# The sixth product of the last two output quads on the second seven-product level

## The chip, the cores and the metric

The kernel runs on one core of a Trainium2 chip. The metric is device time in microseconds (us) of one execution; less is better. The core has a matrix engine (TensorE, PE in the profile, with its weight loads as PEld), a vector engine (VectorE, DVE), a scalar engine (ScalarE, ACT), GpSimd (POOL) and a queue engine (SyncE, SP) that issues most DMAs. Matrix products are accumulated in PSUM, eight banks of 512 float32 columns per partition; everything else lives in SBUF.

## The reference

A linear-attention block and then a token-mixing MLP, each behind a layer norm and with a residual; S = 2048 tokens, D = 1024 channels, F = 3584 hidden units:

```
h  = x + A(layernorm(x), wqkv, wo)                 # attention
u  = gelu(einsum("bsd,sf->bdf", LN(LN(h)), w1) + b1)   # first mixer
y  = einsum("bdf,fs->bds", u, w2) + b2             # second mixer
h2 = h + y.transpose(0, 2, 1)
```

The change is in the second mixer: a product of w2 transposed (2048 x 3584) with the gelu output g (3584 x 1024).

## The kernel before

**Tiling.** The 2048 output rows are 16 tiles of 128; two tiles form a pair p, handled by a `Mixer2` object (`st` in the code); two pairs form a `Quad`. There are four quads, u = 0 to 3. The 3584 hidden units are 14 steps k of two tiles of 128 (even and odd), the 1024 channels two halves of 512 columns.

**First level.** Each pair is a 2 x 2 block product (two row tiles, even and odd hidden tiles, two column halves), done with seven products instead of eight (`Product7`). Product m takes a left operand `lhs[m]` (128 x 128 per k, 14 of them) and a right operand (128 x 512 per k). Operands 1, 2 and 4 are blocks of w2, operands 5, 6, 7 and 3 are sums that VectorE makes (`asum(m)`, 1792 elements per partition): 5 = a21 + a22, 6 = operand 5 - a11, 7 = a11 - a21, 3 = a12 - operand 6. The right operand of product 6 is `gT2`, that of 7 and 4 are `gs` tiles in two halves, parked in DRAM and reloaded, or (second half of 4) made anew by `remake_t4`. In the accumulators: A = P1, then B = P1 + P6, C = B + P7, and so on; A becomes `t1`, a copy of it psB, a copy of that psC (`copy_c`).

**Second level.** Some products are done for both pairs of a quad at once, again as a 2 x 2 block product with seven inner products (`Inner`, and `Inner2`, whose results are added directly where they belong): the two pairs give the two block rows, the parity of k the inner dimension, two halves of 256 columns (HW) the block columns. An inner product is a block of seven matmuls of 256 columns. Its left operands are sums of 896 elements (`Inner.sums`, tiles `is`), its right operands sums of 1792 elements made once and kept (`inner_moving`, tiles `gi`). In quads 1 to 3 the products 1, 5, 2 and 3 are on the second level (stages in1, in5, in2, in3), while 6, 7 and 4 are plain: 14 matmuls of 512 columns for each pair.

**The order around the change.** `Quad.run2` writes out one quad by hand. `Quad.interleave` runs the seven inner products in the order i1, i6, i2, i5, i7, i3, i4 and puts matmuls of a plain product ("fills") between them at four cuts: the second half of the previous quad's product 4 in in1, product 6 in in5, product 7 in in2, the first half of product 4 in in3. At named points between them ("b" after i1, "c" after i6, "2", "7", "third", "end") it emits sums and loads, and flushes `late`, a list of evacuations. The fills cover the way from an inner product through PSUM: i1 is copied by ScalarE to the bank in which i6 accumulates, i6 to the bank for i7 (L273, L279); VectorE or ScalarE reads i2, i5, i7, i3 and i4 (the sinks).

TensorE and VectorE keep the program's order (`Held`, `pin`); ScalarE's order in this part is set by the scheduler. Each engine runs its own queue in order and waits on semaphores. SBUF pools with `reuse_waits="tile"` make a new tile wait only for the tiles whose place it takes. `load("in1")`, after in1, reloads the second half of product 7's `gs` and the odd w2 tiles of the next quad on the SP queue. Outputs go through `out`: an evacuation into one of four small tiles, then an accumulating DMA on POOL's queue.

Of the kernel before, what the change touches and what calls it, by code (L numbers as in the profile page):

```python
# [30 lines left out]
def kernel(  # L31
# [32 lines left out]
    const = ctx.enter_context(tc.tile_pool(name="const", bufs=1))  # L64
    actx_psum = ExitStack()
# [22 lines left out]
    ident = const.tile([P, P], BF16)  # L88
# [26 lines left out]
    b1_rows = const.tile([NF, P], BF16)  # L115
    b2_rows = const.tile([NS, P], BF16)
# [96 lines left out]

    def inner_moving(M, nk, pool, name):
        v = M.rearrange("p (k two) (h f) -> p k two h f", two=2, h=2)
        b11, b12, b21, b22 = v[:, :, 0, 0, :], v[:, :, 0, 1, :], v[:, :, 1, 0, :], v[:, :, 1, 1, :]
        t2, t3, t4 = (pool.tile([P, nk // 2, HW], FP16, name=f"{name}{t}")[:] for t in (2, 3, 4))
# [20 lines left out]
    class Inner:  # L238
# [220 lines left out]
    class Mixer2(Product7):  # L459
# [52 lines left out]
    class Quad:  # L512
# [29 lines left out]
        def interleave(self, n, steps, at={}, flush=(("7", None), ("end", None)), first=0):  # L542
            t = len(steps)
            cuts = [0, (5 * t + 8) // 16 + first, (9 * t + 8) // 16 + first, (12 * t + 8) // 16 + first, t]
# [12 lines left out]
            for f in (  # L557
                n.i1, "b", 0, n.i6, "c", n.i2, "2", 1, n.i5, n.i7, "7", 2, n.i3, "third", 3, n.i4, "end",
            ):
# [38 lines left out]
        def run2(self, rest, nxt, load, sums, cut, first):  # L598
            sts = self.sts

            def starting():
                self.in1.sums(slice(2, 4))
                self.asums(5)
                self.in5 = self.inner(5)
                self.in5.sums(slice(0, 2))
                sts[0].asum(6)
# [3 lines left out]

            def evac(s, dh, t):
                return lambda: sts[s].evac(0, dh, t[:, s, :])

            def every(*fs):
                return lambda: [f() for f in fs]

            def shared(st):
# [18 lines left out]

            def third():
# [1264 lines left out]
```

## Time and profile before

Three runs took 552.0, 552.32 and 553.42 us, median 552.32. The profiled execution took 552.11 us; its span, first to last instruction, is 550.3 us, at a granted TensorE clock of 1.00.

| stretch of the span (us) | what runs | PE busy | DVE busy | ACT busy |
|---|---|---|---|---|
| 0 to 385 | attention, first mixer | 382.80 | 322.63 | 249.47 |
| 385 to 422.19 | quad 0 (plain but product 5) | 37.19 | 33.60 | 6.96 |
| 422.19 to 464.74 | quad 1 | 42.55 | 37.19 | 10.48 |
| 464.74 to 504.26 | quad 2 | 39.52 | 28.26 | 11.53 |
| 504.26 to 547.01 | quad 3 and the last fills | 42.75 | 30.99 | 11.79 |
| 547.01 to 550.3 | last outputs | 0.00 | 0.58 | 0.00 |

The page gives busy times, a chain of the work that ended last, and groups of instructions; the timeline lists instructions in order of time, runs of equal ones merged. Matmul lengths in it are modelled and overlap, so the time a block takes is read from the start of the next one. A VectorE instruction overlaps the next one as well: its price in a full queue is the distance between starts.

### The profile page before, as it was taken

Reading aid. Unit: us, or ns where it says so; the run is one execution under the profiler, and the core shown is the slowest. Engines: PE = TensorE matmul, PEld = TensorE weight load, DVE = VectorE, ACT = ScalarE, POOL = GpSimd, SP = SyncE. Lnnn points to the kernel's source line nnn. Section 1 sums busy time; section 2 is a strip of 40 time slices with the busy share of each in tenths; the row PEclk is TensorE's granted clock in tenths of the full one; section 3 lists DMA queues with packets and bytes.
Section 4 is the critical chain, followed back from the end, with each engine's and each line's share of the span. In section 5 each row is a group of like instructions: output and inputs, shape, how many; then the busy total and the mean of one; then the engine's idle time right before and its main releaser. Section 6 shows DMA issues by size and latency. Waiting matters only on the chain.

```text
span 550.3 us, 9989 instructions
## 1 busy us (share of the span) xinstructions
PE 544.8 (99%) x3888; PEld 322.4 (59%) x3888; DVE 453.2 (82%) x881; ACT 290.2 (53%) x619; POOL 26.3 (5%) x36
## 2 busy tenths in 40 slices
PE   8999999999999999999999999999999999999997
PEld 3444446646634444456666766766455667667665
DVE  7798897865895999879988889888889979749747
ACT  5748677767788777635556465564220413413311
POOL 1000000000000000000000000000002103103111
PEclk9999999999999999999999999999999999999999
DMA  8933432205646981104041340422697749849334
GB/s 290 323 78 76 79 78 40 40 1 154 230 114 180 295 312 76 58 0 155 1 154 59 95 153 2 152 60 77 163 297 199 208 144 235 207 143 218 93 108 74
DMA packets 83151, 74.58 MB, mean 136 GB/s; under 512 B 15890, under 2 KB 74528, under 8 KB 83104
## 3 DMA queue, kind: packets, MB, share of 16 engines
q1 hardware_dynamic: 78720, 69.87, 43.0%
q0 software_dynamic: 4096, 3.68, 4.9%
q8 instruction: 30, 0.49, 0.4%
q10 hardware_dynamic: 288, 0.39, 0.2%
q14 instruction: 17, 0.14, 0.1%
HBM read 59.12 MB, written 11.67 MB: 129 GB/s over the span
## 4 chain that ended last, share of the span: by engine, by line
PE 96%; DVE 1%; DMA 1%; ACT 1%; issue 0%; ACTq 0%; DVEq 0%
PE psI L233 27%; PE psC L233 17%; PE acc_t L233 13%; PE psB L233 11%; PE psC L980 4%; PE psB L980 4%; PE psA L980 4%; PE psA L233 3%; PE acc_t L896 3%; PE psE L980 2%; PE acc_t L1315 2%; PE psA L1114 1%; PE psB L1114 1%; PE psC L1114 1%; PE kvps L926 1%; DMA x_sb<-in_A_x_dram 1%
## 5 line engine op out<-in xcount | busy, mean ns | idle before, releaser
L233 PEld LDWEIGHTS <-is 128*128 128x128 f16 x764 | 74.6, 98 | 32.1 <-DVE hi L233 0.4
L233 PEld LDWEIGHTS <-sa 128*128 128x128 f16 x683 | 66.8, 98 | 34.2
L233 PEld LDWEIGHTS <-wq 128*128 128x128 bf16 (+1 forms) x596 | 58.3, 98 | 38.8 <-issue 1.0
L233 PE MATMUL acc_t<-wo_sb,pqT 128*128 128x512 f16 x256 | 55.6, 379 | 0.0
L490 POOL DMA_DIRECT2D out_dram<-wq x28 | 24.4, 951 | 512.2 <-DMA wq<-in_B_w_dram 391.0
L233 PEld LDWEIGHTS <-pqT 128*128 128x128 bf16 x256 | 25.0, 98 | 30.5 <-issue 0.6
L233 PE MATMUL psC<-gs,wq 128*128 128x512 f16 x168 | 40.8, 379 | 0.0
L233 DVE TENSOR_TENSOR t<-psI,t 128x256 f32<-128x256 f32 (+1 forms) x45 | 20.8, 475 | 22.2 <-PE psI L233 20.9
L980 PEld LDWEIGHTS <-xs 128*128 128x128 f16 x208 | 20.0, 98 | 22.7
L233 PE MATMUL psC<-hT,sa 128*128 128x512 f16 x112 | 31.2, 379 | 0.0
L233 PE MATMUL psI<-hi,is 128*128 128x256 f16 x200 | 30.0, 273 | 0.0
L233 PE MATMUL psB<-hT,sa 128*128 128x512 f16 x112 | 29.7, 379 | 0.0
L233 PE MATMUL psC<-hT,wq 128*128 128x512 f16 x112 | 28.4, 379 | 0.0
L233 DVE BATCH_NORM_STATS2 hst<-acc_t 128x6 f32<-128x512 f32 x32 | 21.1, 690 | 6.9 <-ACT h_bf L233 6.9
L980 PE MATMUL psA<-wkv,xnT 128*128 128x512 bf16 x104 | 26.7, 379 | 0.0
L233 PE MATMUL psB<-gT,sa 128*128 128x512 f16 x112 | 26.5, 379 | 0.0
L980 PEld LDWEIGHTS <-xnT 128*128 128x128 bf16 x156 | 15.2, 98 | 18.1 <-issue 0.2
L233 DVE TENSOR_TENSOR e<-psI,es 128x256 f32<-128x256 f32 x22 | 9.3, 424 | 19.5 <-PE psI L233 19.5
L233 ACT CAST h_bf<-acc_t 128x512 bf16<-128x512 f32 x32 | 18.4, 583 | 12.4 <-PE acc_t L233 12.4
L233 ACT COPY psI<-psI 128x256 f32<-128x256 f32 x50 | 18.0, 360 | 11.6 <-PE psI L233 9.7
L193 DVE TENSOR_SCALAR e_sb<-e_sb 128x512 bf16<-128x512 bf16 x64 | 18.2, 284 | 7.2 <-ACT e_sb L188 7.0
L233 PE MATMUL psI<-gi,is 128*128 128x256 f16 x182 | 24.1, 273 | 0.0
(234 smaller groups left out, 1107.0 us busy)
## 6 DMA issues: line engine op xcount, KB each, us to landing
wq<-in_B_w_dram SPq DMA_DIRECT2D x14, 1024.0 KB, 7.5
wq<-in_B_w_dram SPq DMA_DIRECT2D x20, 448.0 KB, 5.8
gs<-parked SPq DMA_DIRECT2D x9, 896.0 KB, 4.7
shared_sb<-rd_dram SPq DMA_DIRECT2D x32, 128.0 KB, 3.8
out_dram<-h_bf SPq DMA_DIRECT2D x16, 256.0 KB, 3.6
x_sb<-in_A_x_dram SPq DMA_DIRECT2D x14, 256.0 KB, 4.0
w2o<-in_B_w_dram SPq DMA_DIRECT2D x4, 896.0 KB, 9.6
out_dram<-wq POOLq DMA_DIRECT2D x28, 128.0 KB, 4.7
```

Source lines behind the costliest of these rows:

```text
L193: pin(nc.vector.tensor_scalar(e_sb[:], e_sb[:], 1.0, PHI_EPS, ALU.min, ALU.add))
L233: return (lambda *a, **kw: pin(op(*a, **kw))) if self.always or getattr(Held, self.key) else op
L490: nc.gpsimd.dma_start(to, ot[:, a:b], accum_op=ALU.add)
L896: mm = nc.tensor.matmul(pp[:, 0:CW], lhsT=xnT[:, kt, i * P:(i + 1) * P], rhs=wkv[:, kt, c * CW:(c + 1) * CW], start=(kt == 0), stop=(kt == ...
L926: pin(nc.tensor.matmul(kv_ps[q * DH:(q + 1) * DH, j, :], lhsT=pks[i % NPK][:, h * DH:(h + 1) * DH], rhs=vaugs[i % NVA][:, h, :], start=Fal ...
L980: pin(nc.tensor.matmul(ps[:], lhsT=lhs[:, k, :], rhs=rhs[:, k, :], start=(start and k == 0), stop=(k == hk2 - 1), skip_group_check=True,))
L1114: pin(nc.tensor.matmul(out[:, j], lhsT=rhs[:, k, 2 * self.half + j, :], rhs=lhs[:, k], start=(start and j == 0 and k == 0), stop=(k == hk2 ...
L1315: nc.tensor.matmul(qp[:, 0:SW], lhsT=wq_sb[:, kt, j * P:(j + 1) * P], rhs=xnT[:, kt, u * SW:(u + 1) * SW], start=(kt == 0), stop=(kt == ND ...
```

## The change

In quads 2 and 3 product 6 goes to the second level: a new stage in6 between in5 and in2, with `gT2` and sums of it (`gi6`) on the right. psB is no longer a copy of A; VectorE writes it from the inner results and t1 (`sink6`, with a tile `x6` for the part that both pairs share). The 14 fills left from the previous quad's product 4 are spread as 3, 5 and 6 over in1, in5 and in6, and in1 and in6 take a new order ("lean": i1, i6, i5, i7, i2, i3, i4).

SBUF is made for this: three `is` tiles per stage instead of four, the fourth sum overwriting the second after i6; four `is` buffers instead of six; two `sa` buffers instead of four, with sums 6, 7 and 3 in homes that are free by then (the place of a11, a21, of another sum, or of a `gi6` tile); `ident` and the bias rows in a pool that is closed earlier. The four sums of gT2 are made in quads 1 and 2, two each; as they change half of gT2 in place, `remake_t4` takes its correction from its own tile. `load("in1")` comes after in6 in quads 2 and 3. Quad 1 keeps its stages, with sums at other points. In the diff u counts quads, `self.six` is true for 2 and 3.

```diff
     const = ctx.enter_context(tc.tile_pool(name="const", bufs=1))
+    earlyctx = ExitStack()
+    early = earlyctx.enter_context(tc.tile_pool(name="early", bufs=1))
...
-    ident = const.tile([P, P], BF16)
+    ident = early.tile([P, P], BF16)
...
-    b1_rows = const.tile([NF, P], BF16)
-    b2_rows = const.tile([NS, P], BF16)
+    b1_rows = early.tile([NF, P], BF16)
+    b2_rows = early.tile([NS, P], BF16)
...
+    def sum_tile(pool, nk, name):
+        return pool.tile([P, nk // 2, HW], FP16, tag=name, name=name)[:]
...
-                self.sm = [pools[self.tag].tile([P, self.nk, P], FP16, tag=self.tag, bufs=pools["is_bufs"], name="is")[:] for _ in range(4)]
+                self.sm = [pools[self.tag].tile([P, self.nk, P], FP16, tag=self.tag, bufs=pools["is_bufs"], name="is")[:] for _ in range(pools["is_n"])]
+                self.sm += self.sm[1:2] * (4 - pools["is_n"])
...
-        def asum(self, m):
-            if m != 7:
+        def asum(self, m, home=None):
+            if m == 5 or (m == 3 and home is None):
                 return super().asum(m)
-            t = self.a21.bitcast(FP16)
-            self.lhs[7] = t
-            return dve.tensor_tensor(t, self.a11, self.a21, ALU.subtract)
+            if m == 7:
+                self.lhs[7] = self.a21.bitcast(FP16)
+                ks = slice(0, NFP) if home is None else home
+                return dve.tensor_tensor(self.lhs[7][:, ks, :], self.a11[:, ks, :], self.a21[:, ks, :], ALU.subtract)
+            if home is None:
+                t = self.a11.bitcast(FP16)
+            elif isinstance(home, int):
+                t = sum_tile(inner2, NFP, f"gi6{home}").rearrange("p k (two f) -> p (k two) f", f=P)
+            else:
+                t = home
+            a, b = (self.lhs[5], self.a11) if m == 6 else (self.a12, self.lhs[6])
+            self.lhs[m] = t
+            return dve.tensor_tensor(t, a, b, ALU.subtract)
...
+        six = False
+
         def sink1(self, m, h, ps):
             A, B, c = self.sts[m].A, self.sts[m].B, self.cols(h)
             act.copy(A[:, c], ps)
-            act.copy(B[:, c], A[:, c])
+            if not self.six:
+                act.copy(B[:, c], A[:, c])
 
         def sum1(self, m, h, ps, es):
             A, B, c = self.sts[m].A, self.sts[m].B, self.cols(h)
             dve.tensor_tensor(A[:, c], ps, es, ALU.add)
-            act.copy(B[:, c], A[:, c])
+            if not self.six:
+                act.copy(B[:, c], A[:, c])
+
+        def sink6(self, m, h, ps):
+            c = self.cols(h)
+            if isinstance(m, slice):
+                ps = ps.unsqueeze(1).to_broadcast([P, 2, HW])
+                self.x6 = inner2.tile([P, 2, HW], F32, tag="x6", name="x6")
+                dve.tensor_tensor(self.x6[:], ps, self.t1[:, :, c], ALU.add)
+            else:
+                dve.tensor_tensor(self.sts[m].B[:, c], ps, self.x6[:, m, :] if h else self.t1[:, m, c], ALU.add)
...
+        def interleave(self, n, steps, at={}, flush=(("7", None), ("end", None)), first=0, cuts=None, lean=False):
             t = len(steps)
-            cuts = [0, (5 * t + 8) // 16 + first, (9 * t + 8) // 16 + first, (12 * t + 8) // 16 + first, t]
+            order = (n.i1, "b", 0, n.i6, "c", n.i2, "2", 1, n.i5, n.i7, "7", 2, n.i3, "third", 3, n.i4, "end")
+            if cuts is None:
+                cuts = [0, (5 * t + 8) // 16 + first, (9 * t + 8) // 16 + first, (12 * t + 8) // 16 + first, t]
+            else:
+                cuts = [0, *cuts, t]
+            if lean:
+                order = (n.i1, "b", 0, n.i6, "c", n.i5, n.i7, "7", 1, n.i2, "2", 2, n.i3, "third", 3, n.i4, "end")
...
-        def run2(self, rest, nxt, load, sums, cut, first):
...
-                sts[0].asum(6)
+            self.six = not first
+            at1, at5, at6, at2 = {}, {}, {}, {}
...
+            def start_t1():
                 self.t1 = self.base("t1")
                 for s, st in enumerate(sts):
                     st.begin(self.t1[:, s, :])
 
+            def start_in5():
+                self.in5 = self.inner(5)
+                self.in5.sums(slice(0, 2))
+
+            def start_in6():
+                self.in6 = Inner2(sts, 6, self.mov6, "i", self.sink6, None)
+                self.in6.sums(slice(0, 2))
+
+            def start_in2():
+                self.in2 = Inner2(sts, 2, self.mov2, "i", self.add_to(self.t1), None)
+                self.in2.sums(slice(0, 2))
...
-            self.interleave(
-                self.in1, rest, {"b": starting, "7": lambda: self.in5.sums(slice(2, 4)), "third": sums[0]},
-                (("b", None), ("7", None), ("end", None)), first,
-            )
-            load("in1")
-            sts[1].asum(6)
-            sums[1]()
-            e = share(sts)
-            in2 = Inner2(sts, 2, self.mov2, "i", self.add_to(self.t1), None)
-            in2.sums(slice(0, 2))
-            self.interleave(self.in5, self.steps(*[st.p6 for st in sts]), {
-                "b": lambda: sts[0].asum(7), "2": lambda: sts[1].asum(7),
-                "7": lambda: in2.sums(slice(2, 4)), "third": sums[2],
-            })
+            put(at2, "c", summed("in2", 3))
+            put(at5, "c", summed("in5", 3))
+            if self.six:
+                put(at1, "b", start_t1, summed("in1", 2), operand(0, 5))
+                put(at1, "c", summed("in1", 3))
+                put(at1, "7", operand(1, 5))
+                put(at1, "third", start_in5)
+                put(at5, "b", summed("in5", 2), operand(1, 7))
+                put(at5, "c", operand(1, 6))
+                put(at5, "2", lambda: sts[0].asum(6, sts[0].lhs[5]))
+                put(at5, "7", start_in6)
+                put(at5, "third", *sums6[:1])
+                put(at6, "b", summed("in6", 2), *sums6[1:])
+                put(at6, "c", summed("in6", 3))
+                put(at6, "2", operand(0, 7, spans[0]))
+                put(at2, "b", operand(0, 7, spans[1]))
+                put(at6, "third", lambda: sts[0].copy_c(), start_in2)
+                put(at6, "end", lambda: sts[1].copy_c())
+                put(at2, "b", summed("in2", 2), lambda: sts[0].asum(3, sts[0].lhs[6]))
+                put(at2, "2", lambda: sts[1].asum(3, sts[1].lhs[5]))
+                early, flush = (("b", None), ("7", None), ("end", None)), (("7", None), ("end", None))
+                self.interleave(self.in1, rest[:3], do(at1), early, cuts=(3, 3, 3), lean=True)
+                e = share(sts)
+                self.interleave(self.in5, rest[3:8], do(at5), early, cuts=(3, 3, 3))
+                self.interleave(self.in6, rest[8:], do(at6), flush, cuts=(6, 6, 6), lean=True)
+                load("in1")
+            else:
+                put(at1, "b", summed("in1", 2), operand(0, 5), operand(1, 5), operand(0, 6, 2), start_t1)
+                put(at1, "c", summed("in1", 3))
+                put(at1, "7", start_in5)
+                put(at1, "third", sums[0], summed("in5", 2))
+                self.interleave(self.in1, rest, do(at1), (("b", None), ("7", None), ("end", None)), first)
+                load("in1")
+                sts[1].asum(6, 4)
+                sums[1]()
+                e = share(sts)
+                put(at5, "b", operand(0, 7))
+                put(at5, "2", operand(1, 7))
+                put(at5, "7", start_in2)
+                put(at5, "third", sums[2], summed("in2", 2))
+                self.interleave(self.in5, self.steps(*[st.p6 for st in sts]), do(at5))
+                put(at2, "b", operand(0, 3), sums[3], sums6[0])
+                put(at2, "2", operand(1, 3), sums6[1])
...
-            self.interleave(in2, self.pieces(lambda st: st.p7_fill), {
-                "b": every(lambda: sts[0].asum(3), sums[3]), "2": lambda: sts[1].asum(3),
-                "7": lambda: load("p7"), "third": third,
-                "end": lambda: self.late.append(evac(1, 0, self.t1)),
-            }, (("7", None),))
+            put(at2, "third", third)
+            put(at2, "7", lambda: load("p7"))
+            put(at2, "end", lambda: self.late.append(evac(1, 0, self.t1)))
+            self.interleave(self.in2, self.pieces(lambda st: st.p7_fill), do(at2), (("7", None),))
...
             self.interleave(self.in3, p4[:len(p4) // 2], {
-                "b": lambda: self.in3.sums(slice(2, 4)), "2": lambda: load("t4a"), "7": lambda: load("t4b"),
+                "b": lambda: self.in3.sums(slice(2, 3)), "c": lambda: self.in3.sums(slice(3, 4)),
+                "2": lambda: load("t4a"), "7": lambda: load("t4b"),
                 "third": begin_next,
                 "end": lambda: self.late.append(evac(1, 1, e)),
             }, (("b", None), ("7", None)))
...
+    earlyctx.close()
...
-    pools["sa"] = ctx.enter_context(tc.tile_pool(name="sapool2", bufs=4, side="right", reuse_waits="tile"))
+    pools["sa"] = ctx.enter_context(tc.tile_pool(name="sapool2", bufs=2, side="right", reuse_waits="tile"))
...
-    pools["i"], pools["is_bufs"] = inner2, 6
+    pools["i"], pools["is_bufs"], pools["is_n"] = inner2, 4, 3
...
     cur.asum(5)
-    cur.asum(6)
+    cur.asum(6, 2)
     for sl in spans:
         dve.tensor_tensor(gT2[:, sl, :], gO[:, sl, CW:D], gE[:, sl, CW:D], ALU.subtract)
-    cur.asum(3)
+    cur.asum(3, 3)
...
-        k += k % 2
-        even_k = slice(k - H2, o.stop, 2)
-        dve.tensor_tensor(
-            t[:, even_k, HW:CW], t[:, even_k, HW:CW], gO[:, k:H2 + o.stop:2, 0:HW], ALU.add,
-        )
+        even_k = slice(k + k % 2 - H2, o.stop, 2)
+        dve.tensor_tensor(t[:, even_k, HW:CW], t[:, even_k, HW:CW], t[:, even_k, 0:HW], ALU.add)
...
     st.asum(5)
-    st.asum(6)
+    st.asum(6, 4)
...
-    quad.in5.sums(slice(2, 4))
+    quad.in5.sums(slice(2, 3))
     quad.interleave(quad.in5, quad.pieces(lambda st: st.p7_fill), {
-        "b": lambda: (st.asum(3), sums1(slice(0, 2))), "2": lambda: sums1(slice(2, 4)),
+        "b": lambda: (st.asum(3, st.lhs[6]), sums1(slice(0, 2))), "c": lambda: quad.in5.sums(slice(3, 4)),
+        "2": lambda: sums1(slice(2, 4)),
...
+    def start_sums6():
+        Quad.mov6, Quad.sums6 = inner_moving(gT2, NFP, inner2, "gi6")
+        Quad.sums6(slice(0, 1))
+
+    def more_sums6(k):
+        return lambda: Quad.sums6(slice(k, k + 1))
+
     first = quarter(sums2, 0, 2), quarter(sums2, 2, 4), quarter(sums3, 0, 2), quarter(sums3, 2, 4)
+    of_t2 = {1: (start_sums6, more_sums6(1)), 2: (more_sums6(2), more_sums6(3))}
     for u in range(1, NSP // 2):
         rest, nxt = nxt.run2(
-            rest, lambda: next2(u + 1), loads(u), first if u == 1 else (nop,) * 4, CW - P if 2 * u + 2 == NSP else None, 2 if u == 1 else 0,
+            rest, lambda: next2(u + 1), loads(u), first, CW - P if 2 * u + 2 == NSP else None, 2 if u == 1 else 0, of_t2.get(u, ()),
         )
```

More of the change, by code (lines that the diff above doesn't have):

```diff
@@ L216, in inner_moving @@
         b11, b12, b21, b22 = v[:, :, 0, 0, :], v[:, :, 0, 1, :], v[:, :, 1, 0, :], v[:, :, 1, 1, :]
-        t2, t3, t4 = (pool.tile([P, nk // 2, HW], FP16, name=f"{name}{t}")[:] for t in (2, 3, 4))
+        t2, t3, t4 = (sum_tile(pool, nk, f"{name}{t}") for t in (2, 3, 4))
         def sums(part=slice(0, 4)):
@@ L540 @@
         late = []
-        def interleave(self, n, steps, at={}, flush=(("7", None), ("end", None)), first=0):
+        def interleave(self, n, steps, at={}, flush=(("7", None), ("end", None)), first=0, cuts=None, lean=False):
             t = len(steps)
-            cuts = [0, (5 * t + 8) // 16 + first, (9 * t + 8) // 16 + first, (12 * t + 8) // 16 + first, t]
+            order = (n.i1, "b", 0, n.i6, "c", n.i2, "2", 1, n.i5, n.i7, "7", 2, n.i3, "third", 3, n.i4, "end")
[5 more added lines that the diff above has]
+                order = (n.i1, "b", 0, n.i6, "c", n.i5, n.i7, "7", 1, n.i2, "2", 2, n.i3, "third", 3, n.i4, "end")
             flush = dict(flush)
@@ L555, in point @@
                 at.get(name, nop)()
-            for f in (
-                n.i1, "b", 0, n.i6, "c", n.i2, "2", 1, n.i5, n.i7, "7", 2, n.i3, "third", 3, n.i4, "end",
-            ):
+            for f in order:
                 if isinstance(f, int):
@@ L596, in pieces, with run2, put, do @@
             return [(f(st), k) for h in (range(0, H2), range(H2, NFP)) for st in self.sts for k in h]
-        def run2(self, rest, nxt, load, sums, cut, first):
+        def run2(self, rest, nxt, load, sums, cut, first, sums6):
             sts = self.sts
[L601 to L605, printed above, removed]
-                sts[0].asum(6)
+            self.six = not first
+            at1, at5, at6, at2 = {}, {}, {}, {}
+            def put(at, name, *fs):
+                at.setdefault(name, []).extend(fs)
+            def do(at):
+                return {name: lambda fs=fs: [f() for f in fs] for name, fs in at.items()}
+            def summed(which, a, b=None):
+                return lambda: getattr(self, which).sums(slice(a, a + 1 if b is None else b))
+            def operand(s, m, *home):
+                return lambda: sts[s].asum(m, *home)
+            def start_t1():
                 self.t1 = self.base("t1")
@@ L609, in starting @@
                     st.begin(self.t1[:, s, :])
+            def start_in5():
[7 more added lines that the diff above has]
+                self.in2.sums(slice(0, 2))
             def evac(s, dh, t):
                 return lambda: sts[s].evac(0, dh, t[:, s, :])
-            def every(*fs):
-                return lambda: [f() for f in fs]
             def shared(st):
@@ L1443 @@
         pools["i5"] = mctx.enter_context(tc.tile_pool(name="is0", bufs=1, side="right"))
-        pools["is_bufs"] = 4
+        pools["is_bufs"] = pools["is_n"] = 4
         a3p = actx.enter_context(ExitStack())
```

## The prediction

> **What bounds the kernel now.** I read the page first: the busy line, then the chain that ended last.
>
> ```profile
> PE 544.8 (99%) x3888; PEld 322.4 (59%) x3888; DVE 453.2 (82%) x881; ACT 290.2 (53%) x619; POOL 26.3 (5%) x36
> ...
> PE 96%; DVE 1%; DMA 1%; ACT 1%; issue 0%; ACTq 0%; DVEq 0%
> ```
>
> TensorE carries the chain, VectorE is next. Because a busy PE is not a PE at its peak, I next read the timeline of TensorE in the third quad (u=2), which starts at 464.74. Columns: start, modelled length, engine, line, what it does, count.
>
> ```profile
> 464.74 0.93 PE L233 MATMUL psI<-gE,wq 128*128 128x256 f16 x7
> 465.50 1.03 PE L233 MATMUL psC<-gs,w2o 128*128 128x512 f16 x4
> 466.37 0.93 PE L233 MATMUL psI<-gi,is 128*128 128x256 f16 x7
> ...
> 473.11 0.93 PE L233 MATMUL psI<-gE,sa 128*128 128x256 f16 x7
> 473.87 2.11 PE L233 MATMUL psB<-gT,sa 128*128 128x512 f16 x9
> 475.82 0.93 PE L233 MATMUL psI<-gi,is 128*128 128x256 f16 x7
> ...
> 484.50 0.93 PE L233 MATMUL psI<-gO,wq 128*128 128x256 f16 x7
> ```
>
> There is no gap: every block starts as the one before stops issuing. The first stage (in1, 464.74 to 473.11) takes 8.37 us for 49 narrow (256 columns) and 14 wide (512) matmuls; the second (in5, to 484.50) takes 11.39 us for 49 narrow and 28 wide. The difference is 14 wide ones in 3.02 us, so a wide one costs 0.216 us, and 49 narrow ones cost 8.37 - 3.02 = 5.35 us, 0.109 each, a block of seven 0.765. These spacings, not the modelled lengths, price everything on TensorE.
>
> Third, the busy times of the two halves of this quad (us, PE, PEld, DVE, ACT, POOL, clock, DMA):
>
> ```profile
> 464.74:484.50 19.76, 19.76 (x142) 13.70 (x140) 15.55 (x24) 8.21 (x19) 3.45 (x4) 1.00 0.84 214
> 484.50:504.26 19.76, 19.76 (x142) 13.71 (x140) 12.70 (x23) 3.32 (x9) 3.51 (x4) 1.00 0.67 167
> ```
>
> VectorE leaves 4.2 us in the half that the change rewrites. Fourth, its timeline, for prices and for where that idle time lies (in brackets: idle before, and who ended it):
>
> ```profile
> 466.11 0.61 DVE L233 TENSOR_TENSOR is<-wq 128x896 f16<-128x896 bf16 x1
> 466.64 0.62 DVE L233 TENSOR_TENSOR is<-wq,is 128x896 f16<-128x896 bf16 x1
> 467.18 2.09 DVE L233 TENSOR_TENSOR sa<-wq 128x1792 f16<-128x1792 bf16 x2
> ...
> 480.65 0.42 DVE L233 TENSOR_TENSOR e<-psI,es 128x256 f32<-128x256 f32 x1 [3.13 <-PE psI L233]
> ...
> 488.94 0.42 DVE L233 TENSOR_TENSOR t<-psI,t 128x256 f32<-128x256 f32 x1 [5.09 <-PE psI L233]
> ```
>
> From start to next start: an 896-element sum 0.53 (0.65 when the next reads it), a 1792-element sum 1.0, a 256-column PSUM addition 0.34; the same listing gives 0.61 for a 512-column one.
>
> **The change, part by part.**
>
> *TensorE.* In u=2 and u=3 the sixth product stops being 28 wide matmuls and becomes seven blocks of seven narrow ones: 6.04 goes, 5.35 comes, 0.69 saved per quad, 1.38 in both. All other matmuls stay. u=1 keeps the old form.
>
> The rule that speaks against this: the Trainium skill, "TensorE: Matmul & The Clock Gate", section Back-to-back issue gap, calls 131 ns at 512 columns and 81 ns at 128 the sustained spacing. Interpolated, an estimate of 98 ns at 256, that makes 4.8 us against 3.7 and the change 2.2 us slower, about 554.6; the trace shows 216 and 109 ns with no gaps, so I go by the trace.
>
> *VectorE.* Per quad it gains four 896 sums (in6), one 512-column addition into x6 and four 256-column ones into psB; u=2 also takes two 1792 sums of gT2, u=1 the other two. From in1 to in6 (before: in1 and in5) I count, for u=2: 12 sums of 896 at 0.58, 5.5 of 1792 (asum 3 and half of an asum 7 move on to in2) and two for gT2 at 1.0, eight 256-column additions at 0.34, one of 0.61: 17.8. With the 1.37 that the stage before leaves over (464.74 to 466.11) that is 19.2 us, beside 19.08 of TensorE (19.76 - 0.69); u=3 needs 17.2. So VectorE is at its limit and order decides. I lay its queue beside TensorE's, T=0 at in1's first block. A result is read 0.96 after the start of its block of seven (488.94 is 0.97 after 487.97, where that block starts).
>
> TensorE: in1 i1 0, three fills, i6 1.41, i5 2.18, i7 2.94, i2 3.71, i3 4.47, i4 5.24; in5 i1 6.00, i6 7.41, i2 8.18, i5 8.94, i7 9.71, i3 10.47, i4 11.67; in6 i1 12.43, six fills, i6 14.49, i5 15.26, i7 16.02, i2 16.79, i3 17.55, i4 18.32; in2 19.08.
>
> VectorE: in1's third sum 1.37, asum 5 1.90, fourth sum 2.90, addition after i7 3.90, asum 5 4.24, addition after i3 5.43, in5's sums 5.77 and 6.42, third 6.95, asum 7 7.49, fourth 8.49, asum 6 9.02 and 10.02, addition after i7 11.02, in6's sums 11.36 and 12.01, addition 12.54, gT2's third sum 12.88, in6's third 13.89, gT2's fourth 14.42, in6's fourth 15.46, x6 16.22, additions 16.98 and 17.75, half of asum 7 18.09, addition 18.62, in2's two sums 18.96, last addition 20.14.
>
> Where they meet: in5's i6 (7.41) needs the sum that ends at 7.04; in5's i4 (11.67) the addition that ends at 11.44; in6's i6 (14.49) gT2's sum ending at 13.97; the first p7 fill (19.85) C, copied (0.57 in ScalarE's rows) from the addition that ends at 19.04, so 19.65; its eighth step (21.36) the other C, 21.2. All hold, by 0.15 to 0.5. I cost this at nothing; if VectorE slips by s, about s less 0.15 comes back at each meeting.
>
> An addition that writes PSUM has no row on VectorE. Nearest rows: the same addition writing t, 0.42; ScalarE's copy writes PSUM in 0.36 to 0.38, SBUF in 0.37, so a gain is not excluded. Bounds: 0.06 less to 0.27 more (the whole difference of a 512-column one, 0.69) each. I take 0.42, the nearest; the upper end delays C by about 0.5 to 0.8, some 1 to 1.3 for both quads.
>
> The Trainium skill, "Perfetto Trace Analysis", section Optimizing Scalar/DVE Operations, gives VectorE about 125 ns overhead on PSUM and 60 on SBUF; 65 ns more per addition would cost an estimate of 0.1 to 0.2 us per quad. No row here shows it.
>
> *ScalarE.* Four copies into psB go (0.38 each), two between psI banks come (0.36): cheaper. But three fills now stand between i1 and i6 where four and nine stood. The copy starts 0.96 after i1 and takes 0.36, i6 is due at 1.41. The first mixer shows the same spacing without a gap:
>
> ```profile
> 378.39 0.60 PE L233 MATMUL psI<-hO,sa 128*128 128x256 f16 x4
> 378.82 0.81 PE L233 MATMUL psC<-hT,sa 128*128 128x512 f16 x3
> 379.47 0.60 PE L233 MATMUL psI<-hi,is 128*128 128x256 f16 x4
> ```
>
> ```profile
> 379.02 0.36 ACT L233 COPY psI<-psI 128x256 f32<-128x256 f32 x1
> ```
>
> Copy end to i6 0.09, enough; nothing is to spare.
>
> *Added waits.* With three "is" tiles a stage's fourth sum overwrites its second and waits for i6; queued behind it are an asum or an addition, and who needs it is i3, 3 blocks off. asum 6 in the home of asum 5 waits for in5's i2 (result at 9.14; the queue reaches it at 10.02).
>
> *Moved transfers.* The reload of the second gs half and two w2 loads go from after in1 to after in6. The SP queue passes no other issue. The reload starts near T=14.7 instead of 7.9, lands 4.8 later (largest 10.7) and is needed by p7's fifteenth step, the sixth of the second fill, T 24.4: hidden, 0 (at 10.7 it would cost 1.0). The w2 loads (10 to 11.4) are needed in the next quad, 20 us on. POOL's output issues move with their evacuations; nothing waits on them.
>
> *u=0 and u=1.* Same lengths in other homes. u=1's two gT2 sums fall in in2, where before VectorE idles 0.83, 0.85 and 1.39: the additions behind them run up to 1.5 late and the step into in3 is met. remake_t4 keeps its shapes (0.29, 0.43). 0. If that cover is gone the later additions delay in3, at most 1.
>
> *Sum.* 1.38 saved. The profiled execution took 552.11 (span 550.3, 1.8 around it), 0.21 under the median: 550.73 by it, **550.9** by the median 552.32.
>
> **The rivals.**
>
> A, VectorE becomes the bound: 19.2 in 19.1 us speaks for it, the layout above and u=3's 2 us of room against. Missing the four meetings by 0.1 to 0.3 gives back 0.3 to 1.3: 551.3 to 552.3.
>
> B, the other side: an output evacuation on ScalarE (0.72 at 464.70) stands ahead of the copy that i6 waits for, at in1 and in5 of both quads. With no room there each hit costs up to 0.72; more than two of the four (1.44 over 1.38) make the kernel slower, four give 553.8. For it: at 473.7 to 475.0 the copy stood behind an evacuation and two copies, covered by nine fills. Against it: those two copies are removed, and p4's evacuation is then not yet due.
>
> C, the operands of the new stage come so late (or a transfer stalls in2) that nothing is left of the gain: 552.3 and, with the reload at its worst, 553.3.
>
> **How the numbers follow.** 0.3%, about what a measurement of this kernel tells from no change, is 1.66 us: faster means under 550.66, slower above 553.98. Forecast 0.62 (own range 550.4 to 551.3), A 0.17, B 0.13, C 0.08. The clean gain falls 0.28 short of the bound; runs spread over 552.0 to 553.4, so I give 0.16 to a reading beyond it, from the forecast's chance. Slower by 0.3% takes all of B, or B and C together: 0.12. Same 0.72. The range 550.4 to 553.3 leaves out half of B, a part of C and a little below.
>
> **What would show it.** Right: no gaps on TensorE from in1 to in6, in1 6.0, in5 6.4, in6 6.65 us, a quad of 38.8 instead of 39.5, VectorE idle under 1 us before in6's fourth sum. Wrong: a gap ahead of i6 ended by ScalarE (B), ahead of i4 or the first p7 by VectorE or ScalarE (A), ahead of p7's fifteenth step by a DMA (C), or narrow blocks not at 0.765.

## The result and the profile after

The changed kernel takes 551.1 us, the median of 22 runs (550.61 to 552.89), where the kernel before takes 552.15 in 22 runs beside them (551.93 to 553.51). The ratio is 0.9981, with a 95% interval of 0.9974 to 0.9987: 1.05 us less, real, and inside the 0.3% that the prediction set as "the same". Forecast were 550.9 and a range of 550.4 to 553.3.

The profiled execution is a poor one to compare totals with: it took 552.89 us (span 550.9), the longest of the 22. It is good for what happens inside the quads. The page's busy line and its chain:

```profile
PE 544.6 (99%) x3914; PEld 327.6 (59%) x3930; DVE 466.2 (85%) x905; ACT 289.2 (53%) x615; POOL 26.3 (5%) x36
...
PE 95%; DMA 2%; DVE 1%; issue 1%; ACT 0%; ACTq 0%; DVEq 0%
```

TensorE still carries the chain; VectorE has 13 us more to do. A DMA has 2% of the chain now, where it had 1%.

**The stages that were rewritten.** TensorE's timeline of quad 2 (start, modelled length, engine, line, instruction, count; the time of a block is the distance to the next start):

```profile
466.65 0.93 PE L238 MATMUL psI<-gE,wq 128*128 128x256 f16 x7
467.41 0.81 PE L238 MATMUL psC<-gs,w2o 128*128 128x512 f16 x3
468.06 0.93 PE L238 MATMUL psI<-gi,is 128*128 128x256 f16 x7
...
472.64 0.93 PE L238 MATMUL psI<-gE,sa 128*128 128x256 f16 x7
...
479.07 0.93 PE L238 MATMUL psI<-gT,sa 128*128 128x256 f16 x7
479.84 1.46 PE L238 MATMUL psC<-gs,w2o 128*128 128x512 f16 x6
481.13 0.93 PE L238 MATMUL psI<-gi,is 128*128 128x256 f16 x7
...
485.72 0.93 PE L238 MATMUL psI<-gO,wq 128*128 128x256 f16 x7
```

in1 takes 5.99 us (466.65 to 472.64), in5 6.43 (to 479.07), the new in6 6.65 (to 485.72): 19.07 for what took 19.76, with no gap. After in6's i1 (479.07) the next block starts 0.77 later, six fills take 1.29, and i6 starts at 481.13 just when the fills are issued.

The busy times of in1 to in6 of quad 2, the rest of that quad, and in1 to in6 of quad 3 (us; PE, PEld, DVE, ACT, POOL, then clock, DMA share and GB/s):

```profile
466.65:485.72 19.07, 19.07 (x164) 15.76 (x162) 17.94 (x30) 7.15 (x16) 3.45 (x4) 1.00 0.49 124
485.72:505.48 19.76, 19.76 (x142) 13.71 (x140) 16.72 (x30) 4.01 (x8) 3.51 (x4) 1.00 1.03 261
505.48:524.55 19.07, 19.07 (x163) 15.74 (x161) 16.15 (x29) 7.17 (x16) 3.45 (x4) 1.00 0.48 123
```

A quad, from in1 to the next in1, is 38.83 us (466.65 to 505.48) instead of 39.52, and the first three stages of quad 3 show the same 19.07. VectorE went from 15.55 to 17.94 in the rewritten stretch. Its timeline (in brackets: idle before, and who ended it):

```profile
477.69 0.42 DVE L238 TENSOR_TENSOR e<-psI,es 128x256 f32<-128x256 f32 x1
478.03 0.62 DVE L238 TENSOR_TENSOR is<-wq 128x896 f16<-128x896 f16 x1
...
479.55 1.08 DVE L238 TENSOR_TENSOR gi<-gT 128x1792 f16<-128x1792 f16 x1
...
482.86 0.69 DVE L238 TENSOR_TENSOR x<-psI,t 128x512 f32<-128x512 f32 x1
483.66 0.43 DVE L238 TENSOR_TENSOR psB<-psI,x 128x256 f32<-128x256 f32 x1
484.39 0.43 DVE L238 TENSOR_TENSOR psB<-psI,t 128x256 f32<-128x256 f32 x1 [0.30 <-PE psI L238]
```

Less 466.65 these starts are T 11.04, 11.38, 12.90, 16.21, 17.01 and 17.74. The prediction's layout had 11.02, 11.36, 12.88, 16.22, 16.98 and 17.75: the six are met within 0.03, and of the whole list from in1 to in6 the largest difference is 0.07 (the addition after in1's i7 and the sum behind it). The two lines with psB are the addition that had no row before: 0.43 us, against 0.42 for the same addition into e.

ScalarE's timeline at in1 of quads 2 and 3, an output evacuation and then the copy that i6 waits for:

```profile
466.61 0.72 ACT L509 ACTIVATE wq<-e,b_sb 128x512 bf16<-128x512 f32 x1 [5.33 <-DVE e L238]
467.61 0.36 ACT L279 COPY psI<-psI 128x256 f32<-128x256 f32 x1 [0.28 <-PE psI L238]
...
505.58 0.72 ACT L509 ACTIVATE wq<-e,b_sb 128x512 bf16<-128x512 f32 x1 [5.52 <-DVE e L238]
506.44 0.36 ACT L279 COPY psI<-psI 128x256 f32<-128x256 f32 x1
```

The evacuation stands ahead of the copy in both quads and ends 0.28 and 0.14 us before the copy starts, which is 0.96 after i1's start, so it delays nothing.

**Where the profile shows a loss.** Quad 1 was forecast unchanged; in this execution it takes 43.11 us (423.54 to 466.65) instead of 42.55. TensorE stands in its in1:

```profile
423.54 0.93 PE L238 MATMUL psI<-gE,wq 128*128 128x256 f16 x7
424.30 2.54 PE L238 MATMUL psC<-gs,wq 128*128 128x512 f16 x11
427.23 0.94 PE L238 MATMUL psI<-gi,is 128*128 128x256 f16 x7 [0.39 <-DVE is L238]
```

Eleven fills from 424.30 are issued by 426.68, so the gap ahead of i6 is 0.55 (the bracket counts from a modelled end, which lies 0.16 further on). VectorE ended it, and what VectorE had waited for is a load:

```profile
425.89 0.62 DVE L238 TENSOR_TENSOR is<-wq 128x896 f16<-128x896 bf16 x1 [2.49 <-DMA wq<-in_B_w_dram]
426.55 0.62 DVE L238 TENSOR_TENSOR is<-is,wq 128x896 f16<-128x896 f16 x1
```

The queue engine's timeline says why that load is late. In the kernel before:

```profile
408.09 8.72 SPq L233 DMA_DIRECT2D wq<-in_B_w_dram  x4
417.82 0.34 SPq L1752 DMA_DIRECT2D parked<-gs  x1
```

and in the changed one:

```profile
409.43 6.45 SPq L238 DMA_DIRECT2D wq<-in_B_w_dram  x3
417.74 0.34 SPq L1833 DMA_DIRECT2D parked<-gs  x1
418.17 0.39 SPq L238 DMA_DIRECT2D wq<-in_B_w_dram  x1
```

Four loads bring quad 1's even w2 tiles. Now the parking of half of product 4's right operand stands ahead of the fourth. It isn't held in place by the program, so the scheduler chose its place in the queue; it waits there for VectorE to finish that half, and the load is issued behind it.

The other loss is 1.35 us in the first 22 us of the span, far from the change, with VectorE waiting 1.55 us instead of 0.60 for ScalarE's rstd of the first layer norm. Quad 0's in5 starts at 406.96 here, at 405.62 in the kernel before, and between 405.55 and 406.36 in the profiles of the ten runs below. This is a large part of why this execution is long, and it doesn't come back in the two other profiles of this kernel (405.81 and 405.85).

### The profile page after: what moved, and what is told of

Same layout as the page of the kernel before. It is cut to its first block, busy times and chain, and to the rows that moved or that the text cites. A ratio compares the mean times of both kernels' runs of the same rounds, so it can differ in the third digit from the quotient of the medians.

```text
span 550.9 us, 10097 instructions
## 1 busy us (share of the span) xinstructions
PE 544.6 (99%) x3914; PEld 327.6 (59%) x3930; DVE 466.2 (85%) x905; ACT 289.2 (53%) x615; POOL 26.3 (5%) x36
## 3 DMA queue, kind: packets, MB, share of 16 engines
HBM read 59.12 MB, written 11.67 MB: 129 GB/s over the span
## 4 chain that ended last, share of the span: by engine, by line
PE 95%; DMA 2%; DVE 1%; issue 1%; ACT 0%; ACTq 0%; DVEq 0%
PE psI L238 28%; PE psC L238 17%; PE acc_t L238 13%; PE psB L238 7%; PE psC L1060 4%; PE psB L1060 4%; PE psA L1060 4%; PE acc_t L976 4%; PE psA L238 3%; PE psE L1060 2%; PE acc_t L1395 2%; DMA wq<-in_B_w_dram 1%; PE psA L1194 1%; PE psB L1194 1%; PE psC L1194 1%; PE kvps L1006 1%
## 5 line engine op out<-in xcount | busy, mean ns | idle before, releaser
L238 PEld LDWEIGHTS <-is 128*128 128x128 f16 x820 | 80.0, 98 | 32.1 <-DVE is L238 1.1
L238 PEld LDWEIGHTS <-wq 128*128 128x128 bf16 (+1 forms) x610 | 59.7, 98 | 38.6 <-issue 1.0
L238 PEld LDWEIGHTS <-sa 128*128 128x128 f16 x571 | 55.8, 98 | 20.7
L238 PE MATMUL psI<-gi,is 128*128 128x256 f16 x210 | 27.8, 273 | 0.4 <-DVE is L238 0.4
L976 PE MATMUL acc_t<-wkv,xnT 128*128 128x512 bf16 x94 | 22.9, 395 | 0.1
L238 DVE TENSOR_TENSOR sa<-wq 128x2048 f16<-128x2048 bf16 (+1 forms) x17 | 20.0, 1178 | 2.0 <-DMA wq<-in_B_w_dram 2.0
```

What stands on the lines that cost most here:

```text
L238: return (lambda *a, **kw: pin(op(*a, **kw))) if self.always or getattr(Held, self.key) else op
L976: mm = nc.tensor.matmul(pp[:, 0:CW], lhsT=xnT[:, kt, i * P:(i + 1) * P], rhs=wkv[:, kt, c * CW:(c + 1) * CW], start=(kt == 0), stop=(kt == ...
```

## The experiments

Two theories stood against each other on what the change does outside quads 2 and 3. *Queue order*: quads 2 and 3 give all that was forecast, and quad 1 pays in some executions for the load behind the parking. *Shifted start*: quad 1's wait only follows from the slow start of that one execution, or from the new homes of the operands, and costs nothing as a rule. On quads 2 and 3 the question was whether the forecast held by the margins it named, or by luck. "Mended" below is the changed kernel with the edit of the second experiment. Each ratio is to the kernel before on the same chip in the same rounds.

**The changed kernel again**, no edit.

> The changed kernel as it is, a second look. In its first profile quads 2 and 3 took 38.83 and 38.85 us (39.52 and 39.55 before), as forecast, but quad 1 lost 0.55 us where its i6 waited for a left-hand sum that waited for the last w2 load, and the first 22 us lost 1.35. Theory 1: the 0.55 comes from the order of the SP queue (the parking of product 4's first half stands ahead of that load) and is there in every execution; the 1.35 at the start is not and is gone here. Then about 0.83 us faster than before: ratio 0.9985, quad 1 again 0.3 to 0.8 longer than before. Theory 2: both are chance of the memory system; then quad 1 runs without the wait and the ratio is 0.9975.

Measured: 551.29 us, ratio 0.9986 (0.9978 to 0.9995). The profile took 551.08, span 549.1: the loss at the start is gone. The order of the queue and VectorE's wait in quad 1 are still there:

```profile
408.28 6.45 SPq L238 DMA_DIRECT2D wq<-in_B_w_dram  x3
416.63 0.34 SPq L1833 DMA_DIRECT2D parked<-gs  x1
417.06 0.39 SPq L238 DMA_DIRECT2D wq<-in_B_w_dram  x1
```

```profile
423.92 0.63 DVE L238 TENSOR_TENSOR is<-wq 128x896 f16<-128x896 bf16 x1 [1.67 <-DMA wq<-in_B_w_dram]
```

But quad 1 takes 42.55, as before: this expectation was missed. in1 started at 422.38, this sum 1.54 later, and that is early enough. What is early enough can be counted: i6 is due when i1 (0.77) and eleven fills (2.38) are through, at 3.14; ahead of it VectorE needs two sums (0.65 from start to start and 0.62) and 0.06 to hand over. So the first sum may start up to 1.81 after in1, and whatever it is later, TensorE stands. In the first profile it was 2.35, and 2.35 - 1.81 = 0.54 against a gap of 0.55.

**The parking behind the fourth load.**

```diff
-        nc.sync.dma_start(parked[m, h][:], gs[m, h][:])
+        (hd if m == 4 else nc.sync).dma_start(parked[m, h][:], gs[m, h][:])
```

(`hd` issues on the same queue, but keeps the program's order.)

> The changed kernel with one thing put back: the parking of product 4's first half is kept behind the four even w2 loads in the SP queue, as it stood before. Theory 1 (queue order): the last load starts about 0.35 us earlier and shares the DMA engines with nothing of its own queue; VectorE no longer waits for it, or waits under 1 us, TensorE has no gap in quad 1, and the kernel is about 0.55 us faster than the changed one: ratio to the kernel before 0.9975. Theory 2 (chance): same time as the changed kernel.

Measured: 550.95 us (550.62 to 552.28), ratio 0.9979 (0.997 to 0.9988), profile 550.8, span 548.9. The queue and VectorE:

```profile
408.02 8.72 SPq L238 DMA_DIRECT2D wq<-in_B_w_dram  x4
416.83 0.51 SPq L238 DMA_DIRECT2D parked<-gs  x1
```

```profile
422.00 0.63 DVE L238 TENSOR_TENSOR is<-wq 128x896 f16<-128x896 bf16 x1
```

No wait for the load, and quad 1 is 42.55. The wait in quad 1 comes from the order of this queue: with the order alone put back, it is gone. The expected 0.55 us is not in the times: the medians are 0.34 apart and the intervals of the two ratios overlap, as the loss isn't in every execution.

Most of the lateness is not in the issue. The fourth load is issued 5.3 to 5.4 us ahead of in1 in the three profiles of the changed kernel and 5.7 ahead here, so 0.3 to 0.4 later; but it lands 7.6, 6.8 and 6.8 us after its issue there, and 5.5 here (4.8 in the kernel before). Behind the parking its data travel beside the parked 896 KB, twice its own size, issued 0.43 ahead of it; that sharing the DMA engines with it is what slows it is argued, not shown.

**The sixth product plain again, all else as changed.** Product 6 is the 28 wide matmuls again in quads 2 and 3, and the sums of gT2 are not made; the result is computed in full.

```diff
-            self.six = not first
+            self.six = False
...
-    of_t2 = {1: (start_sums6, more_sums6(1)), 2: (more_sums6(2), more_sums6(3))}
+    of_t2 = {u: (nop, nop) for u in (1, 2, 3)}
```

> The changed kernel with product 6 of quads 2 and 3 left plain, as before: no stage in6, no sums of gT2, the old correction in remake_t4; the smaller pools, the homes of the sums and the order in quads 0 and 1 stay. Theory 1: it keeps the loss of about 0.55 us in quad 1 and has no gain: 0.3 to 0.6 slower than the kernel before, ratio 1.0005 to 1.0011. Theory 2 (the loss is chance): 1.0000. If the homes themselves gained something, under 1.

Measured: 552.19 us, ratio 1.0003 (0.9995 to 1.0012); quad 1 takes 42.55, quad 2 39.53. The homes, pools and new order of quads 0 and 1 cost TensorE nothing by themselves. The expected slowdown of 0.3 to 0.6 was missed: the parking stands ahead of the load here too, but VectorE waited for it only 1.01 us (it landed 5.9 after its issue, not 6.8 to 7.6) and its sum started 0.88 after in1, inside the 1.81.

**The parking first, in the kernel before.**

```diff
-    nxt = next2(1, (1,))
+    load_w2(2, 0, hd, spans[1])
     park_half(4, 0)
+    load_w2(3, 0, hd, spans[1])
+    nxt = quad2(1)
```

(with `park_half` held on `hd` as above).

> The kernel before with one thing changed: the parking of product 4's first half is put ahead of the last even w2 load in the SP queue, as the changed kernel has it. There VectorE makes the parked half later beside TensorE than in the changed kernel (417.8 where the last fill of product 7 ends at 416.3), so the load starts 1.7 us later than now. Theory 1: the left-hand sums of quad 1 wait for it and i6 is late by 0.5 to 2 us: ratio 1.001 to 1.0035. Theory 2 (the queue's order does not matter): 1.000.

Measured: 552.4 us, ratio 1.0002 (0.9993 to 1.0011). The profile shows the mechanism in a kernel that has nothing else of the change:

```profile
424.71 0.63 DVE L233 TENSOR_TENSOR is<-wq 128x896 f16<-128x896 bf16 x1 [2.13 <-DMA wq<-in_B_w_dram]
```

in1 started at 422.61, so the sum is 2.10 after it, 0.29 beyond the limit; the gap ahead of i6 is 0.31 and quad 1 takes 42.86 instead of 42.55. The direction is as expected, the size smaller than the 0.5 to 2 expected, and the times don't separate it from nothing.

**The parking ahead of both last loads, in the mended kernel.** `park_half(4, 0)` moved ahead of `next2(1, (1,))`.

```diff
-    nxt = next2(1, (1,))
     park_half(4, 0)
+    nxt = next2(1, (1,))
```

> The kernel of the second experiment (queue mended) with the parking put ahead of both last even w2 loads instead of behind them: the same loss, a larger dose. In the changed kernel the one late load lets VectorE wait 1.7 to 2.5 us, of which TensorE sees 0 to 0.55, so about 2 us of lateness are covered. Queue-order theory: both loads now queue behind the parked half, land 1.5 to 2 us later than there, VectorE waits 3 to 4.5 us and i6 of quad 1 is late by 1.2 to 2.2 us: quad 1 takes 43.8 to 44.8 us instead of 42.55, ratio 0.9997 to 1.0020. Chance theory: quad 1 stays at 42.55, ratio 0.998.

Measured: 551.41 us, ratio 0.9986 (0.9977 to 0.9996).

```profile
408.17 3.42 SPq L238 DMA_DIRECT2D wq<-in_B_w_dram  x2
416.21 0.34 SPq L238 DMA_DIRECT2D parked<-gs  x1
416.64 1.54 SPq L238 DMA_DIRECT2D wq<-in_B_w_dram  x2
```

```profile
424.50 0.63 DVE L238 TENSOR_TENSOR is<-wq 128x896 f16<-128x896 bf16 x1 [2.36 <-DMA wq<-in_B_w_dram]
```

The sum starts 2.23 after in1 and the gap is 0.43 (the limit says 0.42); quad 1 takes 42.99. Expected were 1.2 to 2.2, from a wait of VectorE of 3 to 4.5 us, of which about 2 are covered. The cover was sized well (1.81); the wait was not: it is 2.36. The last load is issued at 417.1 here, as in the changed kernel's second profile (417.06), and lands 7.3 us later instead of 6.8, so a second load behind the parking adds 0.5, not 1.5 to 2.

**One sum more in in5.** In quads 2 and 3 of the mended kernel, in5's third sum is made twice, onto the same tile.

```diff
-                put(at5, "b", summed("in5", 2), operand(1, 7))
+                put(at5, "b", summed("in5", 2), lambda: self.in5.sums(slice(2, 3)), operand(1, 7))
```

> The kernel of the second experiment with in5's third left-hand sum made twice in quads 2 and 3: 0.53 us more on VectorE, the result is the same. My working says VectorE is at its limit from in1 to in6 and that in5's i4 is the meeting with least room (the addition it needs ends at 476.13, i4 starts at 476.33, about 0.1 after the hand-over). So TensorE gets a gap of 0.3 to 0.45 ahead of in5's i4 in each quad, 0.6 to 0.9 in all: ratio 0.9990 to 0.9996. If VectorE has the room that its busy share suggests (17.93 of 19.07 us in quad 2, 16.14 in quad 3): no gap in quad 3, or none at all, ratio 0.998.

Measured: 551.85 us, ratio 0.9997 (0.9987 to 1.0006), 0.9 over the mended kernel. VectorE's and TensorE's timelines ahead of in5's i4 in quad 2:

```profile
476.49 0.41 DVE L238 TENSOR_TENSOR e<-psI,es 128x256 f32<-128x256 f32 x1
```

```profile
476.02 0.59 PE L238 MATMUL psC<-gs,w2o 128*128 128x512 f16 x2
476.96 0.93 PE L238 MATMUL psI<-gi,sa 128*128 128x256 f16 x7 [0.34 <-DVE e L238]
```

The two fills are issued by 476.45; the addition ends at 476.90 and i4 starts 0.06 later: a gap of 0.51, and the same in quad 3, a little over the 0.3 to 0.45 expected. The repeated sum, which writes the tile that the one before it wrote, costs 0.65 from start to start, not the 0.53 of an independent one. So the room at this meeting was 0.65 - 0.51 = 0.14; the prediction had 11.67 - 11.44 = 0.23, less the hand-over, which it left out there. At this meeting VectorE is at its limit in both quads, though it is busy 94% of the stretch in the one and 85% in the other.

**One fill instead of three behind in1's i1** (mended kernel).

```diff
-                self.interleave(self.in1, rest[:3], do(at1), early, cuts=(3, 3, 3), lean=True)
+                self.interleave(self.in1, rest[:3], do(at1), early, cuts=(1, 1, 1), lean=True)
```

> The kernel of the second experiment with one fill between i1 and i6 of in1 in quads 2 and 3 instead of three; the other two follow i3. ScalarE's copy starts 0.97 after i1 and takes 0.36, the hand-over about 0.09, so i6 cannot start before 1.42, and its own place is now 0.98. If my price of that way is right, a gap of 0.4 to 0.45 ahead of i6 in each quad, 0.8 to 0.9 in all, ratio 0.9995; in1 takes 6.4 instead of 6.0 us. If the copy is not what i6 waits for, no gap and 0.998.

Measured: 551.71 us, ratio 0.9989 (0.998 to 0.9999). ScalarE's copy and TensorE in quad 2:

```profile
465.98 0.36 ACT L279 COPY psI<-psI 128x256 f32<-128x256 f32 x1 [0.28 <-PE psI L238]
```

```profile
465.78 0.38 PE L238 MATMUL psC<-gs,w2o 128*128 128x512 f16 x1
466.38 0.92 PE L238 MATMUL psI<-gi,is 128*128 128x256 f16 x7 [0.23 <-ACT psI L279]
```

The copy ends at 466.34, i6 starts 0.04 later; the fill was issued by 466.00: a gap of 0.38 (0.39 in quad 3), a little under the 0.4 to 0.45 expected. Two wide matmuls less ahead of i6 are 0.43 us, so three fills left 0.05 to spare. The forecast's "enough; nothing is to spare" holds, and ScalarE starts the copy as soon as i1 is through.

**The old order of inner products** in in1 and in6 of the mended kernel (`lean=True` removed in both calls).

```diff
-                self.interleave(self.in1, rest[:3], do(at1), early, cuts=(3, 3, 3), lean=True)
+                self.interleave(self.in1, rest[:3], do(at1), early, cuts=(3, 3, 3))
...
-                self.interleave(self.in6, rest[8:], do(at6), flush, cuts=(6, 6, 6), lean=True)
+                self.interleave(self.in6, rest[8:], do(at6), flush, cuts=(6, 6, 6))
```

> The kernel of the second experiment with in1 and in6 in the old order of inner products (i6, i2, i5, i7, i3, i4) with the same fills. By my queue working VectorE's addition after i7 then moves from 3.9 to 4.7 us after i1, the whole queue behind it slips by 0.5 to 0.6 and i6 of in5 waits 0.2 to 0.3, its i4 0.1 to 0.2 more; in6's i4 just holds. So 0.3 to 0.5 per quad, 0.6 to 1.0 in all: ratio 0.9990 to 0.9997. If the order is free, no gaps and 0.998.

Measured: 551.86 us, ratio 0.9992 (0.9982 to 1.0001). Per quad TensorE stands 0.33 ahead of in5's i6 and 0.14 ahead of its i4, both ended by VectorE. The first:

```profile
472.54 0.62 DVE L238 TENSOR_TENSOR is<-is,sa 128x896 f16<-128x896 f16 x1
```

```profile
472.24 0.81 PE L238 MATMUL psC<-gs,w2o 128*128 128x512 f16 x3
473.22 0.94 PE L238 MATMUL psI<-gi,is 128*128 128x256 f16 x7 [0.17 <-DVE is L238]
```

That is 0.47, as expected. In6's i4, which was expected to hold, is 0.05 late as well, and the first three stages take 19.61 us instead of 19.07 in both quads. So 0.54 of the 0.69 per quad hangs on the order of the inner products: where i2 comes before i5 and i7, VectorE's additions, and behind them the sums, come later.

**Changed and mended kernel once more**, both without a further edit, side by side.

> The changed kernel, beside the mended queue on one chip, to tell 0.3 us apart. Queue-order theory: the last w2 load lands 1.7 to 2.5 us late, about 2 us of that are covered, so most executions lose 0 to 0.55 us in quad 1: median 551.1 to 551.3, ratio 0.9981 to 0.9985, and a wider spread than the mended one's. Chance theory: as the mended one.

> The changed kernel with the parking kept behind the four even w2 loads, again. Queue-order theory: no wait of VectorE for the load in quad 1, quad 1 at 42.55 us, quads 2 and 3 0.69 us shorter each: median 550.85 to 550.95, ratio 0.9975 to 0.9979, 0.2 to 0.4 us under the changed kernel. Chance theory: same median as the changed kernel.

Measured: changed 551.25 us, ratio 0.9978 (0.9967 to 0.9988), VectorE's wait 1.64, its sum 1.50 after in1, quad 1 42.54. Mended 550.99, ratio 0.9984 (0.9975 to 0.9992), no wait, quad 1 42.55. Over all runs the changed kernel has a median of 551.19 (44 runs), the mended one 550.99 (22 runs); 27% of the former and 59% of the latter are at 551.0 or below. The intervals of the ratios overlap, and in these last rounds the ratios even stand the other way round, so the times don't separate these 0.2 us. The profiles do show the mechanism: VectorE waits in three of three profiles of the changed kernel, and TensorE pays in one of them; in neither of the two of the mended one. Of the three edited runs above with the mended queue, two show no wait and one (one fill) 0.22 us, which costs TensorE nothing. The mended kernel has the lowest median measured here; that it is faster than the changed one is not shown by the times.

## Why the prediction was right, and where a term was off

- **TensorE, 0.69 saved per quad.** Right: 39.52 became 38.83, and the first three stages 19.07, in both quads. From quad 0's in5 to the end of the span the kernel before takes 144.68 us, the changed and mended profiles without a loss in quad 1 take 143.29 to 143.37: 1.31 to 1.39 less, where 1.38 was summed. The 131 and 81 ns that the Trainium skill ("TensorE: Matmul & The Clock Gate", Back-to-back issue gap) calls sustained are not seen: the narrow blocks stay at 0.765, 109 ns a matmul, and six wide fills take 1.29, 215 ns each.
- **VectorE's queue.** Right, start by start, and its margins are real: one sum more (0.65) opens a gap of 0.51, the old order costs 0.54 a quad. The margins that the layout gave as 0.15 to 0.5 are smaller where they are tightest: 0.14 at in5's i4, and the first copy of C ends at 486.35, 0.13 before the product 7 fill that reads it (486.48). Rival A was one small sum away and did not happen. Reading the order paid; the busy share alone gives no such answer.
- **The addition that writes PSUM.** Taken at 0.42 between 0.36 and 0.69; measured 0.43. Of the higher VectorE cost on PSUM that the Trainium skill names ("Perfetto Trace Analysis", Optimizing Scalar/DVE Operations), none shows between the two destinations: 0.43 against 0.42, and 0.34 from start to start for both.
- **ScalarE's copy.** "Nothing is to spare" was right: 0.05 us. The hand-over to TensorE is 0.04 and not the 0.09 of the row it was read from, which was an upper limit. Rival B did not happen: no copy came late enough to open a gap in either quad. But its order did come about at in1, where the output evacuation ran ahead of the copy in both quads. The prediction's argument against B (two copies are gone, an evacuation is not yet due) is about in5 and doesn't cover in1. There B was 0.28 and 0.14 us away, plus the 0.05, and that it stayed away is luck as far as the prediction goes.
- **The moved reload.** Issued at T 14.68 (forecast 14.7), landing 5.2 later in quad 2 and 4.8 in quad 3 (4.8), no gap from it. Rival C did not happen in quads 2 and 3. Three profiles have a late load that costs TensorE time (the changed kernel's first, and the two runs that move the parking ahead on purpose), but in quad 1, where no rival had placed it.
- **The step that was off: "u=0 and u=1. Same lengths in other homes", put at 0.** ("The SP queue passes no other issue" was said of the moved reload, and holds there; it says nothing of quad 0's queue.) Lengths were indeed the same, and the product 6 part left out gives the time before (ratio 1.0003). But in the changed program the scheduler put the parking ahead of a w2 load, and the term that this adds is 0.55, 0 and 0 us in the three profiles of the changed kernel. In the kernel before, operand 3's sum waits 1.34 us for TensorE, in the changed one, with its new home, it doesn't, and VectorE then begins the half to be parked 1.4 us sooner beside TensorE (414.35, with the 1.35 of the slow start taken off, against 415.78). That this is why the scheduler chose differently was only argued; that its order makes the wait was shown by putting it back.
- **The total.** 550.9 was forecast. The mended kernel takes 550.99, the changed one 551.1 to 551.29. What is left of the 1.38 over the 1.05 measured can be placed by the spans, which are on record for each execution. The median span is 550.4 us in the kernel before (55 executions), 549.2 in the changed kernel (44) and 549.1 in the mended one (22): 1.2 and 1.3 less, so by the spans the parking costs about 0.1 of a median. The rest is time around the span: 1.72 to 1.85 us in every one of the 55, but over 1.85, up to 2.89, in 25 of the 66 executions of the changed and mended kernels. With product 6 plain again it is 1.73 to 1.82 (11 executions). So it seems to come with the new form of product 6; why stays open, and the prediction had taken it as 1.8 unchanged.

## What to carry to other kernels

Lay out the queue of the engine next to the bound beside the bound one, by distances between starts, with the time from result to reader added: here it told gaps of 0.1 to 0.5 us that a busy share of 94% or 85% can't tell. When a buffer gets a new home, look also at every transfer that the program doesn't hold in place: its place in the queue may change, here perhaps because a wait vanished, and a load behind it then comes late. Ask of a late load how long the matmuls already queued cover it, before it is priced by its lateness.

## What the runs showed that was not expected

- In quad 1 the first left-hand sum may start up to 1.81 us after in1 at no cost; beyond that TensorE stands one for one: 2.35, 2.23 and 2.10 gave gaps of 0.55, 0.43 and 0.31; 1.54, 1.50 and 0.88 gave none.
- A VectorE result is read by TensorE 0.05 to 0.06 us after it ends, in the places shown where it was late; a ScalarE result 0.04 after.
- Two sums in a row that write one tile are 0.65 us apart, like two of which one reads the other (478.03 and 478.68 in the changed kernel), where independent ones are 0.53 apart.
- With product 6 on the second level, 25 of 66 executions take 1.86 to 2.89 us outside the span, where all 55 of the kernel before take 1.72 to 1.85.
